# Ten operations for an inverse root, and other places for three writes and for four kinds of loads, in a fused S4 and gMLP kernel on one core

## The chip, the core and the metric

The kernel runs on one core of one Trainium2 chip. The core has a matrix engine (PE), a vector engine (DVE), an activation engine (ACT), a general engine (POOL) and a queue engine (SP). PE writes into eight accumulation banks (PSUM); DVE and ACT read the banks and work on the on-chip memory. Transfers to and from the chip's main memory are issued by SP, ACT or POOL and carried by 16 shared DMA engines. Every engine works through its own instructions in order and waits for the others by semaphores. The metric is the device time of one execution in microseconds.

## The reference, cut to what matters

```python
def _B_ref(x, w_in, w_sp, b_sp, w_out):
    z = _gelu(jnp.einsum("bsd,df->bsf", x, w_in))
    z1 = z[..., :Fh]
    z2 = _layernorm(z[..., Fh:], axis=-1)
    g = jnp.einsum("ts,bsf->btf", w_sp, z2) + b_sp[None, :, None]
    return jnp.einsum("bsf,fd->bsd", z1 * g, w_out)

mod = (_silu(c) @ w_mod).reshape(c.shape[0], 6, 1, -1)
sa, ca, ga, sb, cb, gb = (mod[:, 0], mod[:, 1], mod[:, 2], mod[:, 3], mod[:, 4], mod[:, 5])
h = _layernorm(x, axis=-1) * (1 + ca) + sa
x = x + ga * _A_ref(h, ...)          # S4: 576 channels, 128 poles each, a convolution over 2048 tokens
h = _layernorm(x, axis=-1) * (1 + cb) + sb
x = x + gb * _B_ref(h, ...)          # 2048 tokens, w_in 576 x 4608, w_sp 2048 x 2048, w_out 2304 x 576
```

Every layer norm is `(x - m) / sqrt(v + 1e-5)`: the inverse root is what `rsqrt` computes.

## The kernel before

**Stages.** The first stage (`ssm`) computes the S4 branch; its order is a list written out by hand (`ORDER`). It writes x1, the input of the second half, to main memory (`x1_d`, shown as `x_d`) by channel chunks; the last 64 channels of tokens block 4 to 15 also stay on chip in `x1l`. The **token stage** (`phase_a`) takes the 2048 tokens in 16 blocks of 128: layer norm, transpose, product with the z2 half of w_in (`z2_mm`, five parts per block), GELU, the mean and variance of z2 over all 2304 columns (`z2_stats`), its inverse root (`roots`), the normed z2 (`z2_norm`) and its store (`z2_store`, shown as `z_d<-z`). Beside these run pieces of work that the third stage needs (`side`): w_in's z1 half is scaled, split in two 16-bit parts and stored (`win_d`), w_sp and w_out are measured, and the first seven of the eight w_sp row blocks of token block 0 are split into a high and a low part (`wsp_hi` on ACT, `wsp_lo` on DVE). The **third stage** (`phase_b`) takes the output tokens in four blocks of 512. In each, z1 is computed, w_sp is multiplied with z2 (`g_products`: products of sums in the manner of Strassen, each operand split in two 16-bit parts, so that three products stand for one), the gate is formed, and w_out is applied (`out_block`).

**What sets the order.** In the token stage and the third stage DVE, ACT, PE and SP follow the order in which the Python code issues instructions; POOL is free. `tied` means just that. The token loop runs in a fixed pattern per block; `side(b, k, ...)` hangs a piece of work at place k of block b: LD at its start, V0 after the first statistics, A1 after the third product, V1 before the last statistics.

**The end of the token stage.** After block 15 come `z2_stats(15, 5)`, `roots(15)`, `z2_norm(15)` and `z2_store(15)`. Then the first block of the third stage starts: five units of z1 (`z1_unit`, 14 products each, with a tile `wf` that `z1_load` brings from `win_d`; four tiles stand ready, the fifth takes the place of the first when that has been used), then `g_products` with sets of z2 (`z2_load` into a buffer `raw`, `z2_sums` on DVE, `z2_hi` on ACT, `z2_lo` on DVE into `zset`). There are four buffers `raw` and three `zset`.

**The change to the second block.** `out_block` goes over eight halves n = 0..7 (two column halves of four token tiles). For each it takes the next section of the generator `next_steps`, issues 54 products of w_out into two banks, and has the result summed (`out_sum`: one ACT copy, then three DVE operations on `ot`, the last of which also reads the x1 tile `xo` or `gt`; after every second one ACT issues the store to `out`). The sums of halves 0 to 2 come together after half 2, and the halves 1 and 2 take no section: there are six calls, and six sections. The sections prepare the next block: sums of the w_sp row blocks 1 to 7 (`step_sums(n, ("b", i))`, on DVE, with the ACT split behind them), their low parts (`step_lo`), their loads (`block_read`), and, for the second block alone (n = 1), the first set of the z1 weights (`("w", 0)`: loaded by `item_load`, four transfers of 128 KB, into `raw`; split into `zset`), and loads of further sets (`item_load`, a call that does nothing for n = 2 and 3). A buffer goes to the request that follows the earliest release in program order.

**rsqrt.** It starts from an integer estimate and takes three Newton steps, each instruction waiting for the one before, on tiles of 1 to 4 columns. It is called four times in `ssm` (`ln_stats`), once for the first three token blocks (`ln2_three`), and 16 times by `roots`.

In the trace, `bsz` are the statistics of z2, `vh`, `rq` and `rx` the tiles of `rsqrt`, `xz` the w_sp row blocks of the token stage, `nt` the transposed normed tokens, `ps` and `pz` the banks. Since a helper records every instruction of DVE, ACT, PE and SP, all have line L224.

Of the kernel before, what the change touches and what calls it, by code (L numbers as in the profile page):

```python
# [14 lines left out]
ALU = mybir.AluOpType  # L15
# [3 lines left out]
D = 576  # L19
# [8 lines left out]
CHL = CHW[-1]  # L28
# [872 lines left out]
def rsqrt(V, pool, r, var, n):  # L901

    vh = pool.tile([128, n], F32, name="vh%d" % n)
    q = pool.tile([128, n], F32, name="rq%d" % n)
    V.tensor_scalar(vh, var, 1e-5, 0.5, op0=ALU.add, op1=ALU.mult)
    V.tensor_single_scalar(q.bitcast(I32), vh.bitcast(I32), 1, op=ALU.logical_shift_right)
    V.tensor_scalar(r.bitcast(I32), q.bitcast(I32), -1, 0x5F3759DF - 0x400000, op0=ALU.mult, op1=ALU.add)

    for i in range(3):
        V.tensor_tensor(q, r, r, op=ALU.mult)  # L910
        V.tensor_tensor(q, q, vh, op=ALU.mult)
        if i < 2:
            V.scalar_tensor_tensor(r, q, 1.5, r, op0=ALU.subtract, op1=ALU.mult)
    V.tensor_scalar(q, q, -1.0, 1.5, op0=ALU.mult, op1=ALU.add)
    V.tensor_tensor(r, r, q, op=ALU.mult)


class Mixed:
# [7 lines left out]
class Mlp:  # L926
# [376 lines left out]

    def x1_load(self, b):
        xt = self.xts[b] = self.ap.tile([128, D], F32, name="x1t")
        self.nc.sync.dma_start(xt[:, :D - CHL], self.x1_d[b, :, :D - CHL])

    def ln2_stats(self, b, mv=None):
        V, ap = self.nc.vector, self.ap
        if b < 4:  # L1310
            self.xts[b] = self.x1f[:, b]
        else:
            V.tensor_copy(self.xts[b][:, D - CHL:], self.x1l[:, b - 4])
        x = self.xts[b]
        bs = ap.tile([128, 2, 6], F32, name="bsx")
        mv = self.mvx[b] = ap.tile([128, 2, 2], F32, name="mvx") if mv is None else mv
        for h in range(2):
            V.bn_stats(bs[:, h], x[:, 288 * h:288 * h + 288])
        V.bn_aggr(mv[:, 0], bs)
# [102 lines left out]
    def phase_a(self):  # L1422
# [16 lines left out]
        LD, PE, A0, A1, V0, V1 = range(6)  # L1439
        sides = [[[] for _ in range(6)] for _ in range(17)]  # L1440

        def side(b, k, fn, *a):
            sides[b][k].append((fn, a))
# [31 lines left out]
        for i in range(7):  # L1475
            side(9 + i, V0, self.wsp_sums, i)
            side(9 + i, A1, self.wsp_hi, 0, i)
            side(9 + i, V1, self.wsp_lo, 0, i)
            side(8 + i, V1, self.block_load, 0, i)
        side(12, LD, self.z1_rows, 0)  # L1480
        side(14, LD, self.bias_load, 0)
        for f, b in ((0, 14), (9, 15), (1, 15), (10, 15)):
            side(b, LD, self.z1_load, 0, f)


# [71 lines left out]
        cpa.close()  # L1557
        self.z2_stats(15, 5)
        self.roots(15)
        self.z2_norm(15)  # L1560
        self.z2_store(15)
        self.nc = plain
# [319 lines left out]
    def out_block(self, q, steps):  # L1882


        nc = self.nc
        A, S = nc.scalar, nc.sync
        halves = [(tt, h) for tt in range(4) for h in range(2)]
        pms = {}
        for n, (tt, h) in enumerate(halves):
            if n not in (1, 2):  # L1890
                next(steps)
            pms[tt, h] = [self.bank()[:, :288] for _ in range(2)]
            self.out_products(pms[tt, h], q, tt, h, range(8) if n < 3 else range(9))
            for k in range(3) if n == 2 else () if n < 2 else (n,):
                tt, h = halves[k]
                if n == 2:
                    self.out_products(pms[tt, h], q, tt, h, (8,))
                xt = self.wss["x", tt]
                self.out_sum(pms[tt, h], xt, q, h)
                b, hs = 4 * q + tt, slice(288 * h, 288 * h + 288)  # L1900
                if h == 1:
                    A.dma_start(self.out[b], xt)

    def last_products(self, pm, k, s, fs):
        T = self.nc.tensor
        pa, pl = pm
        for f in fs:
            p, w = self.prods[3, f][k], self.wlast(k, f)
            c, st, sp = slice(128 * s, 128 * s + 128), f == 0, f == 8
            T.matmul(pl, p[:, 1, c], w[:, 0], start=st, stop=sp)  # L1910
            T.matmul(pa, p[:, 0, c], w[:, 0], start=st, stop=False)
            T.matmul(pa, p[:, 0, c], w[:, 1], start=False, stop=sp)
# [145 lines left out]
    def next_steps(self, q, pg):  # L2058

        n = q + 1  # L2060
        gate = self.g_unit(q, 8, pg, 2)
        gate[0]()
        self.scale_gate(q)
        gate[1]()
        gate[2]()
        if q < 3:
            self.n2_adds(1, self.wss["n2", 1])
            self.block_read(n, 3)
        gate[3]()
        gate[4]()  # L2070
        if q == 3:
            return
        self.bias_load(n)
        self.step_hi(n, 1)
        self.step_sums(n, ("b", 1))
        self.rows_load(q, 1)
        self.step_lo(n, ("n", 1))
        self.step_sums(n, ("b", 2))
        self.step_lo(n, ("b", 1))
        self.block_read(n, 4)  # L2080
        self.block_read(n, 5)
        self.wr_scale(0)
        if n > 1:
            self.feed(n, 0)
            self.feed(n, 1)
        yield
        self.step_sums(n, ("b", 3))
        self.step_lo(n, ("b", 2))
        self.block_read(n, 6)
        self.step_sums(n, ("b", 4))  # L2090
        self.step_lo(n, ("b", 3))
        self.block_read(n, 7)
        self.rows_load(q, 2)
        yield
        self.step_sums(n, ("b", 5))
        self.step_lo(n, ("b", 4))
        self.item_load(n)
        yield
        self.step_sums(n, ("w", 0) if n == 1 else ("b", 6))
        self.step_lo(n, ("b", 5))  # L2100
        self.item_load(n)
        self.rows_load(q, 3)
        yield
        if n == 1:
            self.step_sums(n, ("b", 6))
            self.step_lo(n, ("w", 0))
        self.step_sums(n, ("b", 7))
        self.step_lo(n, ("b", 6))
        if n == 1:
            self.item_load(n)  # L2110
            self.feed(n, 1)
        yield
        self.step_lo(n, ("b", 7))
        self.item_load(n)
        self.item_load(n)
        self.item_sums(n, 3)
        yield
# [344 lines left out]
```

## Time and profile before

| what | value |
|---|---|
| runs | 1701.16, 1702.41 and 1707.59 us, median 1702.41 us |
| the profiled execution | 1696.56 us, of which 1694.1 us are the span |
| PE busy | 1620.3 us of the span |
| DVE busy | 1308.0 us |
| ACT busy | 873.0 us |
| moved by DMA | 380.35 MB, 225 GB/s on average |
| granted PE clock, mean | 0.986 |

The stages, by the time from the span's start: the first stage to about 384 us, the token stage to about 613 us, the first block of the third stage to about 889 us, and three more blocks to the end. The profile's columns: the time at which an instruction (or a run of like ones) starts, its duration, the engine, the operation, the tile that is written and those that are read, the shape; in square brackets, how long the engine had been idle before and what ended the wait. PEld is PE's load of weights, SPq and ACTq are queue instructions.

### The profile page before, as it was taken

To read this page: it belongs to the slowest core of one execution; us is meant where nothing else is said; L and a number is where in the kernel's file an instruction comes from. 1 tells how busy PE (TensorE), PEld (TensorE's weight loads), DVE (VectorE), ACT (ScalarE), POOL (GpSimd) and SP (SyncE) were. 2 spreads that over 40 slices of the span, in tenths; PEclk is the share of its full clock that TensorE was granted. 3 is DMA by queue.
4 is the path that set the end of the run, shared out by engine and by line. 5 is a ranking of instruction groups with operands and counts; after the bars stand their busy time and mean duration, and the time that the engine had idled before them with its cause. 6 is when DMAs were issued, how large, how long until landed. Compare 5 with 4: busy or idle time off the path is not lost.

```text
span 1694.1 us, 39997 instructions
## 1 busy us (share of the span) xinstructions
PE 1620.3 (96%) x16868; PEld 1238.2 (73%) x16868; DVE 1308.0 (77%) x2312; ACT 873.0 (52%) x1307; POOL 210.1 (12%) x340
## 2 busy tenths in 40 slices
PE   3788999989999999999999999999999999999999
PEld 1345677755555557778878888888888888888887
DVE  7998999867999977988987777785443387787555
ACT  6989999665776664554443533332321133353221
POOL 3261111112222110000000000000111100111100
PEclk9878999999999999999999999999999999999999
DMA  9667645696988788676748877665667573777560
GB/s 242 178 214 224 198 143 179 174 308 196 281 278 251 237 260 300 242 274 227 248 126 281 292 275 258 221 208 189 224 213 242 190 227 121 270 283 253 191 237 29
DMA packets 186402, 380.35 MB, mean 225 GB/s; under 512 B 38464, under 2 KB 105792, under 8 KB 185456
## 3 DMA queue, kind: packets, MB, share of 16 engines
q1 hardware_dynamic: 145216, 181.84, 35.0%
q0 software_dynamic: 34528, 169.11, 29.7%
q10 hardware_dynamic: 6480, 26.86, 4.0%
q8 instruction: 132, 2.16, 0.5%
q14 instruction: 46, 0.38, 0.1%
HBM read 272.47 MB, written 105.29 MB: 223 GB/s over the span
## 4 chain that ended last, share of the span: by engine, by line
PE 37%; issue 31%; DVE 12%; ACT 4%; DMA 4%; POOL 3%; SPq 0%; ACTq 0%; POOLq 0%; DVEq 0%
PE ps L224 21%; PE pz L224 10%; POOL zset L2158 3%; DMA zset<-set_d 2%; PE pk_b L224 2%; DVE zset L224 2%; PE pk_a L224 2%; DVE raw L224 1%; PE pk_c L224 1%; DVE gt L224 1%; PE pk_d L224 1%; DVE wsp L224 1%; DVE bsz L224 1%; ACT wsp L224 1%; DVE ot L224 1%
## 5 line engine op out<-in xcount | busy, mean ns | idle before, releaser
L224 PEld LDWEIGHTS <-zset 128*128 128x128 f16 x7182 | 701.8, 98 | 91.7 <-DVE zset L224 4.6
L224 PE MATMUL ps<-wsp,zset 128*128 128x256 f16 x6048 | 667.7, 273 | 4.0 <-DVE ot L224 1.5
L224 PE MATMUL pz<-wz,nt 128*128 128x512 f16 (+1 forms) x1120 | 220.9, 358 | 2.1 <-DVE nt L224 0.9
L224 ACT ACTIVATE z<-gt 128x1024 f16<-128x1024 f32 x56 | 59.0, 1054 | 255.9 <-DVE gt L224 255.9
L224 PEld LDWEIGHTS <-nt 128*128 128x128 f16 x1120 | 109.3, 98 | 107.9 <-DVE nt L224 1.8
L2158 POOL DMA_DIRECT2D zset<-set_d x96 | 50.8, 529 | 865.0 <-PE ps L224 614.8
L224 DVE SCALAR_TENSOR_TENSOR gt<-ps,sc,bsp 128x512 f32<-128x512 f32 x36 | 27.0, 749 | 144.5 <-PE ps L224 142.8
L224 PE MATMUL ps<-wout,z 128*128 128x288 f16 x1092 | 138.4, 286 | 0.0
L224 PEld LDWEIGHTS <-z 128*128 128x128 f16 x1176 | 115.1, 98 | 28.9
L224 DVE TENSOR_TENSOR raw<-raw 128x256 f32<-128x256 f32 (+3 forms) x238 | 126.8, 539 | 11.0 <-DMA raw<-z_d 4.1
L224 PE MATMUL ps<-n2o,zset 128*128 128x256 f16 x1134 | 128.4, 273 | 1.8 <-DVE zset L224 1.8
L224 DVE SCALAR_TENSOR_TENSOR gt<-ps,sc,gt 128x512 f32<-128x512 f32 (+1 forms) x180 | 122.2, 696 | 7.9 <-DVE gt L224 0.5
L224 ACT ACTIVATE zset<-raw 128x1792 f16<-128x1792 f32 x48 | 81.0, 1690 | 55.9 <-PE ps L224 17.8
L224 DVE TENSOR_TENSOR zset<-raw,zset 128x1792 f16<-128x1792 f32 x48 | 96.9, 2019 | 16.1 <-ACT zset L224 16.1
L224 DVE TENSOR_TENSOR z<-ps,z 128x512 f32<-128x512 f32 (+1 forms) x126 | 71.9, 598 | 36.3 <-ACT z L224 24.2
L224 ACT ACTIVATE z<-pz,sc 128x512 f32<-128x512 f32 (+1 forms) x96 | 51.2, 574 | 33.9 <-PE pz L224 19.5
L224 ACT ACTIVATE wsp<-raw,sc 128x1792 f16<-128x1792 f32 x25 | 44.6, 1784 | 46.2 <-DVE raw L224 37.2
L224 ACT ACTIVATE z<-z,sc 128x1024 f32<-128x1024 f32 x21 | 24.1, 1149 | 76.0 <-DVE z L224 72.2
L224 ACT ACTIVATE z1b<-gt 128x512 f16<-128x512 f32 (+1 forms) x22 | 17.7, 821 | 85.3 <-DVE gt L224 85.3
L224 PE MATMUL ps<-n2q,wf 128*128 128x512 f16 x252 | 55.9, 379 | 1.2 <-DMA wf<-win_d 1.2
L224 DVE SCALAR_TENSOR_TENSOR wsp<-raw,sc,wsp 128x1792 f16<-128x1792 f32 x25 | 51.9, 2077 | 0.0
L224 POOL DMA_DIRECT2D z_d<-z x32 | 32.2, 1006 | 150.7 <-ACT z L224 149.7
(795 smaller groups left out, 2813.2 us busy)
## 6 DMA issues: line engine op xcount, KB each, us to landing
zset<-set_d POOLq DMA_DIRECT2D x96, 896.0 KB, 5.3
raw<-z_d SPq DMA_DIRECT2D x48, 512.0 KB, 5.6
set_d<-zset ACTq DMA_DIRECT2D x24, 896.0 KB, 6.4
z_d<-z POOLq DMA_DIRECT2D x32, 576.0 KB, 8.8
zset<-wa_d POOLq DMA_DIRECT2D x18, 896.0 KB, 4.8
raw<-in_w_spT SPq DMA_DIRECT2D x25, 512.0 KB, 4.3
set_d<-zset SPq DMA_DIRECT2D x12, 896.0 KB, 5.9
wst<-in_w_in SPq DMA_DIRECT2D x8, 1024.0 KB, 9.5
```

Source lines behind the costliest of these rows:

```text
L224: return self.tc.keep_in_program_order(f(*a, **k))
L2158: self.nc.gpsimd.dma_start(o, self.set_d[f, j - 1] if j else self.wa_d[f])
```

## The change

Five things change.

1. `rsqrt` makes its first two Newton steps in one of higher order and then one Newton step: ten operations instead of thirteen.
2. Token blocks 8 to 15 load all 576 columns of x1 from main memory; the copy of 64 columns from `x1l` on DVE remains for blocks 4 to 7 alone. Eight copies go.
3. The low part of w_sp row block 6, the last that the token stage splits (`wsp_lo(0, 6)`), moves from its place V1 in block 15 to behind `roots(15)`.
4. The first four `z1_load` are asked for at blocks 12, 13, 13 and 14 instead of 14, 15, 15 and 15.
5. `next_steps` gets a seventh section, which `out_block` takes after its last sum. Row block 7 is loaded one section later, and its low part and the sums of set 3 come in the seventh section. For the second block the first z1 weights are asked for earlier, and their low part is made right behind the low part of row block 5.

```diff
@@ -906,13 +906,13 @@
     V.tensor_single_scalar(q.bitcast(I32), vh.bitcast(I32), 1, op=ALU.logical_shift_right)
     V.tensor_scalar(r.bitcast(I32), q.bitcast(I32), -1, 0x5F3759DF - 0x400000, op0=ALU.mult, op1=ALU.add)
 
-    for i in range(3):
-        V.tensor_tensor(q, r, r, op=ALU.mult)
-        V.tensor_tensor(q, q, vh, op=ALU.mult)
-        if i < 2:
-            V.scalar_tensor_tensor(r, q, 1.5, r, op0=ALU.subtract, op1=ALU.mult)
-    V.tensor_scalar(q, q, -1.0, 1.5, op0=ALU.mult, op1=ALU.add)
-    V.tensor_tensor(r, r, q, op=ALU.mult)
+    V.tensor_tensor(q, r, r, op=ALU.mult)
+    V.scalar_tensor_tensor(q, q, math.sqrt(1.5), vh, op0=ALU.mult, op1=ALU.mult)
+    V.scalar_tensor_tensor(q, q, 2.5 / math.sqrt(1.5), q, op0=ALU.subtract, op1=ALU.mult)
+    V.scalar_tensor_tensor(r, q, 1.875, r, op0=ALU.add, op1=ALU.mult)
+    V.tensor_tensor(q, r, r, op=ALU.mult)
+    V.scalar_tensor_tensor(q, q, -1.0, vh, op0=ALU.mult, op1=ALU.mult)
+    V.scalar_tensor_tensor(r, q, 1.5, r, op0=ALU.add, op1=ALU.mult)
 
 
 class Mixed:
@@ -1303,13 +1303,14 @@
 
     def x1_load(self, b):
         xt = self.xts[b] = self.ap.tile([128, D], F32, name="x1t")
-        self.nc.sync.dma_start(xt[:, :D - CHL], self.x1_d[b, :, :D - CHL])
+        n = D if b >= 8 else D - CHL
+        self.nc.sync.dma_start(xt[:, :n], self.x1_d[b, :, :n])
 
     def ln2_stats(self, b, mv=None):
         V, ap = self.nc.vector, self.ap
         if b < 4:
             self.xts[b] = self.x1f[:, b]
-        else:
+        elif b < 8:
             V.tensor_copy(self.xts[b][:, D - CHL:], self.x1l[:, b - 4])
         x = self.xts[b]
         bs = ap.tile([128, 2, 6], F32, name="bsx")
@@ -1475,11 +1476,12 @@
         for i in range(7):
             side(9 + i, V0, self.wsp_sums, i)
             side(9 + i, A1, self.wsp_hi, 0, i)
-            side(9 + i, V1, self.wsp_lo, 0, i)
+            if i < 6:
+                side(9 + i, V1, self.wsp_lo, 0, i)
             side(8 + i, V1, self.block_load, 0, i)
         side(12, LD, self.z1_rows, 0)
         side(14, LD, self.bias_load, 0)
-        for f, b in ((0, 14), (9, 15), (1, 15), (10, 15)):
+        for f, b in ((0, 12), (9, 13), (1, 13), (10, 14)):
             side(b, LD, self.z1_load, 0, f)
 
 
@@ -1557,6 +1559,7 @@
         cpa.close()
         self.z2_stats(15, 5)
         self.roots(15)
+        self.wsp_lo(0, 6)
         self.z2_norm(15)
         self.z2_store(15)
         self.nc = plain
@@ -1900,6 +1903,7 @@
                 b, hs = 4 * q + tt, slice(288 * h, 288 * h + 288)
                 if h == 1:
                     A.dma_start(self.out[b], xt)
+        next(steps)
 
     def last_products(self, pm, k, s, fs):
         T = self.nc.tensor
@@ -2089,29 +2093,31 @@
         self.block_read(n, 6)
         self.step_sums(n, ("b", 4))
         self.step_lo(n, ("b", 3))
-        self.block_read(n, 7)
+        self.item_load(n)
         self.rows_load(q, 2)
         yield
         self.step_sums(n, ("b", 5))
         self.step_lo(n, ("b", 4))
-        self.item_load(n)
+        self.block_read(n, 7)
         yield
         self.step_sums(n, ("w", 0) if n == 1 else ("b", 6))
         self.step_lo(n, ("b", 5))
-        self.item_load(n)
+        if n == 1:
+            self.step_lo(n, ("w", 0))
+            self.item_load(n)
         self.rows_load(q, 3)
         yield
         if n == 1:
             self.step_sums(n, ("b", 6))
-            self.step_lo(n, ("w", 0))
         self.step_sums(n, ("b", 7))
         self.step_lo(n, ("b", 6))
         if n == 1:
             self.item_load(n)
+            self.item_load(n)
             self.feed(n, 1)
         yield
+        yield
         self.step_lo(n, ("b", 7))
-        self.item_load(n)
         self.item_load(n)
         self.item_sums(n, 3)
         yield
```

What stands in a row on the engines that the prediction speaks of, at three places:

DVE at the end of the token stage, before: the statistics of block 15 (`bsz`), the low part of the w_sp row block 6 (`wsp<-xz`), the last two statistics, and the start of the last `rsqrt`.

```order
L224 BN_STATS bsz<-z_7713 128x6
L224 BN_STATS bsz<-z_7714 128x6
L224 SCALAR_TENSOR_TENSOR wsp<-xz,sc,wsp 128x7x256
L224 BN_STATS bsz<-z_7714 128x6 x2
L224 BN_AGGR mvx<-bsz 128x2
L224 TENSOR_SCALAR vh_7826<-mvx 128x1
```

DVE at the same place now, from the middle of the last `rsqrt` on; `r` and `nm` are the scale and shift that `z2_norm(15)` reads, and `raw` the sums of the first set of z2.

```order
L224 TENSOR_TENSOR rq_7758<-rx 128x1
L224 SCALAR_TENSOR_TENSOR rq_7758<-rq_7758,vh_7757 128x1
L224 SCALAR_TENSOR_TENSOR rx<-rq_7758,rx 128x1
L224 TENSOR_SCALAR r_7769<-rx 128x1
L224 SCALAR_TENSOR_TENSOR nm_7770<-mvx,r_7769 128x1
L224 SCALAR_TENSOR_TENSOR wsp<-xz,sc,wsp 128x7x256
L224 TENSOR_TENSOR raw<-raw 128x256
L224 TENSOR_TENSOR raw<-raw 128x512
```

The low part has moved from ahead of the last statistics to between the last `rsqrt` and the first sums of z2.

DVE at the change to the second block, before: the low part of row block 6, the sum of half 6, the low part of row block 7, the sums of set 3 and the sum of half 7.

```order
L224 SCALAR_TENSOR_TENSOR wsp<-raw,sc,wsp 128x7x256
L224 TENSOR_TENSOR ot<-ot,ps 128x288
L224 TENSOR_TENSOR ot<-ot,gbs 128x288
L224 TENSOR_TENSOR gt<-ot,gt 128x288
L224 SCALAR_TENSOR_TENSOR wsp<-raw,sc,wsp 128x7x256
L224 TENSOR_TENSOR raw<-raw 128x256
L224 TENSOR_TENSOR raw<-raw 128x512
L224 TENSOR_TENSOR ot<-ot,ps 128x288
L224 TENSOR_TENSOR ot<-ot,gbs 128x288
L224 TENSOR_TENSOR gt<-ot,gt 128x288
```

The same place now.

```order
L224 SCALAR_TENSOR_TENSOR wsp<-raw,sc,wsp 128x7x256
L224 TENSOR_TENSOR ot<-ot,ps 128x288
L224 TENSOR_TENSOR ot<-ot,gbs 128x288
L224 TENSOR_TENSOR gt<-ot,gt 128x288
L224 TENSOR_TENSOR ot<-ot,ps 128x288
L224 TENSOR_TENSOR ot<-ot,gbs 128x288
L224 TENSOR_TENSOR gt<-ot,gt 128x288
L224 SCALAR_TENSOR_TENSOR wsp<-raw,sc,wsp 128x7x256
L224 TENSOR_TENSOR raw<-raw 128x256
L224 TENSOR_TENSOR raw<-raw 128x512
```

The two sums of halves 6 and 7 follow each other, and row block 7's low part and set 3's sums come behind them. Earlier on the same engine, the low part of the first z1 weights (`zset<-raw,sc,zset`) now stands right behind the low part of row block 5, ahead of the sum of half 5 and the sums of row block 6.

SP at the change to the second block, before (-) and now (+): `in_w_spT` are row blocks of w_sp, `in_w_in` the z1 weights, `x_d` the x1 tiles, `wa_d` the store of the split z1 weights, `z_d` a set of z2.

```order
-L224 DMA raw<-in_w_spT 128x2x512 x4
-L224 DMA xo<-x_d 128x576
-L224 DMA raw<-in_w_in 128x2x128 x4
-L224 DMA raw<-z_d 128x1024
-L224 DMA gt<-x_d 128x576
-L224 DMA wa_d<-zset 128x3584
+L224 DMA raw<-in_w_spT 128x2x512 x3
+L224 DMA raw<-in_w_in 128x2x128 x4
+L224 DMA xo<-x_d 128x576
+L224 DMA raw<-in_w_spT 128x2x512
+L224 DMA wa_d<-zset 128x3584
+L224 DMA raw<-z_d 128x1024
```

The z1 weights now come ahead of the x1 tile `xo` and of the last row block. PE, ACT and POOL execute what they executed, in the same order.

## The prediction

> **What bounds the kernel now.** I read the head of the page first, then the table of stretches (columns: stretch, its length, busy us and instructions of PE, PEld, DVE, ACT and POOL, granted clock, DMA share, GB/s), then the timeline at the stretches in which PE is not full.
>
> ```profile
> span 1694.1 us, 39997 instructions
> PE 1620.3 (96%) x16868; PEld 1238.2 (73%) x16868; DVE 1308.0 (77%) x2312; ACT 873.0 (52%) x1307; POOL 210.1 (12%) x340
> ...
> PEclk9878999999999999999999999999999999999999
> ```
>
> ```profile
> 42.00:384.00 342.00, 308.02 (x6301) 206.96 (x6299) 304.16 (x482) 297.31 (x534) 80.06 (x126) 0.93 0.68 202
> 384.00:556.00 172.00, 171.39 (x916) 90.26 (x917) 156.21 (x478) 118.68 (x192) 40.58 (x55) 1.00 0.80 250
> 556.00:645.00 89.00, 86.72 (x498) 48.32 (x497) 74.15 (x191) 55.09 (x73) 12.25 (x14) 1.00 0.85 261
> 645.00:836.00 191.00, 190.05 (x1565) 152.72 (x1564) 165.91 (x195) 92.12 (x83) 0.57 (x1) 1.00 0.74 256
> 836.00:900.00 64.00, 60.72 (x500) 48.68 (x499) 57.44 (x84) 24.94 (x25) 0.55 (x1) 1.00 0.51 164
> 900.00:1094.00 194.00, 192.84 (x1747) 170.40 (x1746) 142.96 (x189) 77.71 (x93) 11.63 (x22) 1.00 0.80 275
> 1094.00:1694.00 600.00, 595.84 (x5271) 515.32 (x5268) 376.02 (x606) 178.74 (x259) 47.58 (x90) 1.00 0.60 204
> ```
>
> PE bounds the kernel: it is idle for 1694.1 - 1620.3 = 73.8 us in all, and no PE instruction is added or removed. The most that the edits can bring is the idle time of PE where they work: 89.00 - 86.72 = 2.28 us at the end of the token stage (556 to 645) and 64.00 - 60.72 = 3.28 us at the change to the second block (836 to 900). Before 556 PE is full, so the roots and copies there are hidden. Only in the first stage is something else open: PE, DVE and ACT are all at 87 to 90% from 42 to 384.
>
> **Cost of one root.** The rows are one of the 16 calls of `roots` (its first operation, its last, and the one that follows) and the start of the last call.
>
> ```profile
> 565.04 0.17 DVE L224 TENSOR_SCALAR vh<-mvx 128x2 f32<-128x2 f32 x1
> ...
> 567.42 0.16 DVE L224 TENSOR_TENSOR rx<-rx,rq 128x2 f32<-128x2 f32 x1
> 567.61 0.15 DVE L224 TENSOR_SCALAR r<-rx 128x1 f32<-128x1 f32 x1
> ...
> 620.76 0.15 DVE L224 TENSOR_SCALAR vh<-mvx 128x1 f32<-128x1 f32 x1
> ```
>
> Thirteen operations take 567.61 - 565.04 = 2.57 us, 0.198 us each, chained. I price the new fused operations at the same pitch, since the fused ones in this run (`rx<-rq,rx`) keep it too. Three fewer give **0.59 us** a call. [...]
>
> **End of the token stage.**
>
> ```profile
> PE pz L224 <- DVE nt L224: 0.9, 2, 0.5
> ```
>
> ```profile
> 560.63 0.18 DVE L224 COPY x1t<-x1l 128x64 f32<-128x64 f32 x1
> 560.72 0.81 DVE L224 BATCH_NORM_STATS2 bsx<-x1t 128x6 f32<-128x288 f32 x2
> ...
> 607.35 1.41 SPq L224 DMA_DIRECT2D wf<-win_d  x3
> ...
> 616.43 0.32 SPq L224 DMA_DIRECT2D wf<-win_d  x1
> ...
> 617.36 2.08 DVE L224 SCALAR_TENSOR_TENSOR wsp<-xz,sc,wsp 128x1792 f16<-128x1792 f32 x1 [1.12 <-ACT wsp L224]
> ...
> 623.71 2.59 ACT L224 ACTIVATE z<-z,nm,r 128x1152 f32<-128x1152 f32 x2 [5.44 <-DVE nm L224]
> ...
> 626.71 3.20 PE L224 MATMUL ps<-n2q,wf 128*128 128x512 f16 x14 [1.25 <-DMA wf<-win_d]
> ...
> 627.91 2.03 DVE L224 TENSOR_TENSOR zset<-raw,zset 128x1792 f16<-128x1792 f32 x1 [3.24 <-ACT zset L224]
> ...
> 634.23 0.32 SPq L224 DMA_DIRECT2D raw<-z_d  x1
> ```
>
> From 556 on the chain of waits runs through DVE and ACT, not PE, so their savings add up there. Five calls of `roots` start from there on, one a token block, the first and the last those of 565.04 and 620.76: 5 x 0.59 = 2.95 us. Two of the eight copies lie here; the next instruction starts 0.09 us after one starts, so they bring 0.2 us. DVE then reaches `nt` over 0.6 us earlier at its two waits (0.6 us for the first: the roots of 565 and the copy of 561), and the **0.9 us** that PE waits for `nt` go. The fifth `wf` was issued at 616.43, when the first had been used, and landed at about 626.7, behind three others issued at 607.35 on the same queue. These three, 0.96 MB, leave that place; at the stretch's 261 GB/s they are 3.7 us of traffic, more than the **1.25 us** that PE waits. PE then starts the first z2 products some 2.2 us earlier, at 629.9 - 2.2 = 627.7.
>
> What would be late next is the first `zset`. Its sums stand behind the moved write as they did before, so that move is neutral for them, and they come 2.95 + 0.2 = 3.1 us earlier: the DVE write of 627.91 starts at 624.8 and ends at 626.8, 0.9 us ahead of PE. The norm of block 15 gains 2.08 us more, less what it then waits for its GELU (between 0 and 1.1 us), so the set load blocked until 634.23 by the store goes out some 4 us earlier. Without that cover each microsecond of a late set costs PE one. Term: **2.3 us**, the whole idle time; bounds 0.9 (only the `nt` waits go) and 2.3. The wider x1 loads are 8 x 32 KB more, below 1 us of DMA spread over eight blocks, on a core whose DMA share is 0.80: nothing.
>
> **Change to the second block.**
>
> ```profile
> 874.29 0.42 SPq L224 DMA_DIRECT2D xo<-x_d  x1
> ...
> 878.99 1.91 SPq L224 DMA_DIRECT2D raw<-in_w_in  x4
> ...
> 882.53 0.89 DVE L224 TENSOR_TENSOR raw<-raw 128x256 f32<-128x256 f32 x2 [2.02 <-DMA raw<-in_w_in]
> ...
> 889.24 2.08 DVE L224 SCALAR_TENSOR_TENSOR zset<-raw,sc,zset 128x1792 f16<-128x1792 f32 x1
> ...
> 891.37 4.54 PE L224 MATMUL ps<-n2o,zset 128*128 128x256 f16 x40 [1.80 <-DVE zset L224]
> ...
> 896.35 2.08 DVE L224 SCALAR_TENSOR_TENSOR wsp<-raw,sc,wsp 128x1792 f16<-128x1792 f32 x1
> ...
> 899.40 0.45 DVE L224 TENSOR_TENSOR ot<-ot,ps 128x288 f32<-128x288 f32 x1
> 899.90 5.29 PE L224 MATMUL ps<-wsp,zset 128*128 128x256 f16 x47 [1.48 <-DVE ot L224]
> 900.37 0.46 DVE L224 TENSOR_TENSOR gt<-ot,gt 128x288 f32<-128x288 f32 x1
> ...
> 901.38 1.70 ACT L224 ACTIVATE zset<-raw 128x1792 f16<-128x1792 f32 x1 [6.13 <-DMA raw<-in_w_in]
> ...
> xo<-x_d SPq DMA_DIRECT2D x1, 288.0 KB, 4.3
> ```
>
> Here DVE is the late one: it waits 2.02 us for the z1 weights, and PE waits 1.80 us for their low part and 1.48 us for a bank that the sum of half 7 holds. The weights are now asked for after row block 3's low part instead of row block 4's, 5 us earlier (at about 874 by the `xo` row, which followed at the same release), so the 2.02 us go. Their low part also passes the sum of half 5 (1.4 us) and row block 6's sums (1.5 us): 889.24 - 2.02 - 2.9 = 884.3, done at 886.4, 3 us before PE asks at 889.6. The 1.80 us go. The sum of half 7 passes row block 7's low part and set 3's sums (899.40 - 896.35 = 3.05 us): 899.40 - 2.02 - 3.05 = 894.3, its bank free at 894.8. PE, 1.80 us earlier, wants it at 896.6: the 1.48 us go too. Queued behind: `xo` is issued 1.9 us later, behind the four (1.91 us of issue), and lands 4.3 us after that, at 874.3 + 1.9 + 4.3 = 880.5, about when DVE reads it; a stall there of up to 0.5 us lies inside these margins. Late next is set 3: its ACT part stood at 901.38, behind the store of half 7; now its sums end at about 899 and its low part at 902.9 (1.70 and 2.02 us), while PE wants it about 84 products after 894.8, at some 904: a margin of 1 us. Term: **3.3 us**, bounds 2.0 (only DVE's wait is won) and 3.3.
>
> At the other two changes the moved write costs nothing, because DVE waits there:
>
> ```profile
> 1162.26 0.45 DVE L224 TENSOR_TENSOR ot<-ot,ps 128x288 f32<-128x288 f32 x1 [1.51 <-ACT ot L224]
> ```
>
> **First stage.**
>
> ```profile
> L224 DVE TENSOR_TENSOR rq<-rq,vh x15: 161/161/164, 26.8 to 376.4; 128x4 f32<-128x4 f32 x12, 128x3 f32<-128x3 f32 x3
> ...
> 384.25 1.02 DVE L224 TENSOR_TENSOR nt<-pt,nt 128x512 f16<-128x512 f32 x2 [5.14 <-ACT nt L224]
> ...
> 140.00:160.00 20.00, 18.07 (x529) 11.25 (x528) 14.22 (x18) 19.22 (x39) 2.81 (x4) 0.88 0.67 214
> ```
>
> The product with `vh` comes three times a call: four calls on 4 columns, 4 x 0.59 = 2.4 us of DVE. The call on 3 columns ends ahead of DVE's pause of 5.14 us and brings nothing. From 140 to 160 ACT is the full engine and DVE waits, so part is lost; bounds 0 and 2.4, and I take **1.0**.
>
> **Sum.** 2.3 + 3.3 + 1.0 = 6.6 us. The profiled execution took 1696.56 us (span plus 2.5), so its like would take 1690.0. The runs shown lie higher, at a median of 1702.41; the forecast is 1702.4 - 6.6 = **1695.8 us**, 0.39% less. A measurement tells about 0.5%, or 8.5 us, from no change. Bounds of the terms: 0.9 + 2.0 + 0 = 2.9 to 2.3 + 3.3 + 2.4 = 8.0 us.
>
> **Rivals.** (a) *Everything comes through*: the first stage gives its 2.4 us, and of the 1.16 us of PE's idle time from 900 to 1094 (waits for sets) some goes too: 8.0 to 9.2 us, about 1694 us. For it: DVE is above 90% busy in most of the first stage. Against: ACT and PE are too. Chance 0.17. (b) *Traffic, not order, is late*: the fifth `wf` and the sets wait for bytes, and moving three loads changes nothing.
>
> ```profile
> 612.00:620.00 8.00, 8.00 (x45) 4.21 (x44) 6.38 (x11) 5.83 (x7) 2.00 (x2) 1.00 1.06 329
> ```
>
> The DMA engines are full there. Then 1.25 us stay, and set 3's margin breaks as well: 0.9 + 2.0 = 2.9 to 4 us, about 1699. Against: the three loads leave this stretch for one where the share is lower. [...] Chance 0.15. (c) *The clock takes it back*: the granted clock was 0.93 from 42 to 384 and 1.00 after; were the fuller PE throttled by 1% over the 1049 us from 645 on, it would lose 10.5 us, and the time would be 1706, slower. It decides from 0.6%. Against: PE is full from 645 to 836 at 1.00. Chance 0.05. (d) *The edits don't reach PE*: DVE is held by ACT at both places, and nothing beyond 1 us is won, 1701.5. Chance 0.06. The forecast, 4 to 8 us, has 0.57.
>
> The range takes in (a), (b) and most of (d), and the runs' spread: 1689 to 1702. Faster by over 0.5%: (a) and a little of the forecast, 0.20. Slower: 0.04. Within: 0.76.
>
> **What would show it.** Right: no PE wait for `nt` or `wf` between 550 and 640, none for `zset` or `ot` around 890, no DVE wait for `in_w_in`, ten operations at 0.198 us. Wrong: a PE wait for `zset` in the first products of either block, DVE waiting for `xo` at half 4, a clock below 1.00 after 340, or a first stage that ends later than 384.

## The result, and the profile after

| | runs | median | lowest to highest |
|---|---|---|---|
| before | 6 | 1703.03 us | 1701.16 to 1707.59 us |
| changed | 6 | 1693.95 us | 1691.0 to 1697.43 us |

The ratio is 0.995 (95% interval 0.9932 to 0.9968), so 9.1 us less, or 5.4 to 11.6 us by the interval. The forecast was 1695.8 us, 6.6 us less. A second set of runs of the same kernel gave 1694.37 us beside 1704.19 us, a ratio of 0.9951 (0.9935 to 0.9967).

The profiled execution took 1691.0 us. The head of its page, and then its table of the same stretches as before (length, busy us and instructions of PE, PEld, DVE, ACT and POOL, granted clock, DMA share, GB/s):

```profile
span 1688.9 us, 39922 instructions
...
PE 1615.6 (96%) x16868; PEld 1235.7 (73%) x16868; DVE 1298.4 (77%) x2241; ACT 873.8 (52%) x1307; POOL 209.7 (12%) x340
```

```profile
42.00:384.00 342.00, 304.30 (x6308) 203.66 (x6306) 302.54 (x470) 296.54 (x532) 78.26 (x124) 0.95 0.68 202
384.00:556.00 172.00, 170.48 (x906) 89.40 (x907) 151.69 (x440) 118.33 (x191) 40.18 (x55) 1.00 0.82 255
556.00:645.00 89.00, 88.70 (x518) 50.56 (x517) 72.80 (x173) 57.92 (x77) 14.26 (x16) 1.00 0.91 268
645.00:836.00 191.00, 190.03 (x1569) 153.07 (x1568) 165.39 (x196) 91.32 (x83) 0.60 (x2) 1.00 0.73 253
836.00:900.00 64.00, 64.00 (x535) 52.08 (x533) 57.34 (x84) 26.79 (x28) 1.04 (x2) 1.00 0.54 170
900.00:1094.00 194.00, 192.81 (x1749) 170.58 (x1748) 146.15 (x194) 78.68 (x94) 11.10 (x21) 1.00 0.79 272
1094.00:1689.00 595.00, 590.86 (x5227) 511.08 (x5224) 371.74 (x600) 175.95 (x256) 47.58 (x90) 1.00 0.60 205
```

PE's idle time has gone from 2.28 us to 89.00 - 88.70 = 0.30 us at the end of the token stage and from 3.28 us to nothing at the change to the second block. From 645 to 836 and behind 900 it is as before. Ahead of 556 it is longer (37.70 us for 33.98 from 42 to 384, and 1.52 for 0.61 from 384 to 556): the first stage lies otherwise in this execution, as shown below. DVE has 71 instructions fewer: 63 of the 21 roots and eight copies.

The spans alone differ by 5.2 us, the medians by 9.1 us. To see why, I cut each trace at three points of PE: the first z2 product (the end of the first stage), and the first w_out product of the first and of the second block. The rows of the timeline (start, duration, engine, operation, tiles, shape, count) are, of before and then of the changed kernel:

```profile
384.10 2.76 PE L224 MATMUL pz<-wz,nt 128*128 128x512 f16 x12 [0.69 <-ACT nt L224]
...
836.27 0.90 PE L224 MATMUL ps<-wout,z 128*128 128x288 f16 x6
...
1108.94 2.25 PE L224 MATMUL ps<-wout,z 128*128 128x288 f16 x17
```

```profile
385.78 1.04 PE L224 MATMUL pz<-wz,nt 128*128 128x512 f16 x4 [0.69 <-ACT nt L224]
...
835.23 2.00 PE L224 MATMUL ps<-wout,z 128*128 128x288 f16 x15
...
1104.13 1.14 PE L224 MATMUL ps<-wout,z 128*128 128x288 f16 x8
```

All kernels of this study, cut in the same way, in us (the last column is the sum of the three stretches behind the first stage):

| kernel | first stage ends | token stage and first block | change to the second block | rest | behind the first stage |
|---|---|---|---|---|---|
| before | 384.10 | 452.17 | 272.67 | 585.17 | 1310.0 |
| changed | 385.78 | 449.45 | 268.90 | 584.78 | 1303.1 |
| changed, again (e5) | 388.87 | 449.00 | 268.59 | 584.98 | 1302.6 |
| e1, roots alone | 386.26 | 448.97 | 272.70 | 585.05 | 1306.7 |
| e2, second block alone | 388.74 | 452.25 | 268.77 | 585.11 | 1306.1 |
| e3, loads alone | 396.26 | 452.24 | 272.03 | 584.88 | 1309.2 |
| e4, roots and loads | 389.67 | 449.01 | 271.42 | 584.90 | 1305.3 |
| e6, without copies and moved write | 389.77 | 449.40 | 268.84 | 584.96 | 1303.2 |
| e7, old roots in first stage | 390.40 | 450.87 | 270.31 | 584.77 | 1306.0 |
| e8, long roots in first stage | 397.05 | 448.99 | 268.23 | 584.88 | 1302.1 |
| e9, early load alone | 394.25 | 452.45 | 269.32 | 584.91 | 1306.7 |
| e10, order without it | 389.55 | 453.37 | 270.37 | 584.78 | 1308.5 |
| e11, roots and second block | 387.83 | 448.99 | 268.74 | 584.77 | 1302.5 |
| e12, loads behind | 389.42 | 448.98 | 269.97 | 585.47 | 1304.4 |

Behind the first stage the change brings 1310.0 - 1303.1 = 6.9 us: 2.7 in the first block, 3.8 at the second, 0.4 in the rest. The first stage itself ended 1.7 us later in the changed kernel's trace. It is the stage that differs most from execution to execution: the profiled execution of before, at 384.1, has the shortest first stage of all 14 traces, and its 1696.56 us lie below all six timed runs. So the spans show less than the medians.

What the root, the first sets and the second block look like now, in rows of the timeline of the changed kernel (the start and the end of one root, PE's five z1 units and the first z2 sets, then the second block):

```profile
578.91 0.17 DVE L224 TENSOR_SCALAR vh<-mvx 128x2 f32<-128x2 f32 x1
...
580.89 0.15 DVE L224 TENSOR_SCALAR r<-rx 128x1 f32<-128x1 f32 x1
...
614.15 15.27 PE L224 MATMUL ps<-n2q,wf 128*128 128x512 f16 x70
...
626.20 2.02 DVE L224 TENSOR_TENSOR zset<-raw,zset 128x1792 f16<-128x1792 f32 x1 [1.81 <-ACT zset L224]
...
629.26 3.00 PE L224 MATMUL ps<-wsp,zset 128*128 128x256 f16 x26
```

```profile
872.81 1.90 SPq L224 DMA_DIRECT2D raw<-in_w_in  x4
...
879.03 0.46 DVE L224 TENSOR_TENSOR xo<-ot,xo 128x288 f32<-128x288 f32 x1
...
882.99 2.08 DVE L224 SCALAR_TENSOR_TENSOR zset<-raw,sc,zset 128x1792 f16<-128x1792 f32 x1
...
888.15 4.75 PE L224 MATMUL ps<-n2o,zset 128*128 128x256 f16 x42
...
892.73 1.03 PE L224 MATMUL ps<-n2r,wr 128*128 128x256 f16 x6
893.02 0.46 DVE L224 TENSOR_TENSOR gt<-ot,gt 128x288 f32<-128x288 f32 x1 [0.28 <-DMA raw<-in_w_in]
893.40 0.45 DVE L224 TENSOR_TENSOR ot<-ot,ps 128x288 f32<-128x288 f32 x1
...
899.77 2.02 DVE L224 TENSOR_TENSOR zset<-raw,zset 128x1792 f16<-128x1792 f32 x1 [1.89 <-ACT zset L224]
```

The five units run without a gap, the first set is done at 626.20 + 2.02 = 628.22, 1.0 us before PE takes it, and the first products of the second block follow each other without a wait. The 0.28 us that DVE waits at 893.02 stand ahead of an operation that reads `gt` and not the z1 weights: `gt` was asked for at 886.0 and took 6.9 us to land, so it is the likely cause, though the profile names `in_w_in`.

### The profile page after: what moved, and what is told of

It is laid out like the page before. It is cut to its first block, busy times and chain, and to the rows that moved or that the text cites. A ratio compares the mean times of both kernels' runs of the same rounds, so it can differ in the third digit from the quotient of the medians.

```text
span 1688.9 us, 39922 instructions
## 1 busy us (share of the span) xinstructions
PE 1615.6 (96%) x16868; PEld 1235.7 (73%) x16868; DVE 1298.4 (77%) x2241; ACT 873.8 (52%) x1307; POOL 209.7 (12%) x340
## 4 chain that ended last, share of the span: by engine, by line
PE 77%; DVE 7%; DMA 3%; issue 2%; ACT 2%; SPq 0%; POOL 0%; ACTq 0%; DVEq 0%; POOLq 0%
PE ps L224 58%; PE pz L224 10%; PE pk_b L224 2%; PE pk_a L224 2%; DMA zset<-set_d 2%; PE pk_c L224 2%; PE pk_d L224 1%; DVE zset L224 1%; DVE gt L224 1%; DVE bsz L224 1%; PE ps_a L224 0%; PE ps_b L224 0%; DMA v_d<-v_a 0%; PE pt L224 0%; DMA uu_a<-in_x 0%
## 5 line engine op out<-in xcount | busy, mean ns | idle before, releaser
L224 DVE BATCH_NORM_STATS2 bsz<-z 128x6 f32<-128x384 f32 x96 | 48.4, 548 | 5.0 <-ACT z L224 4.4
```

What stands on the lines that cost most here:

```text
L224: return self.tc.keep_in_program_order(f(*a, **k))
```

## Experiments

### The end of the token stage: which part brings it (e1, e3, e4)

e1 has the ten-operation root alone, e3 the earlier loads alone, e4 both:

```diff
-        for f, b in ((0, 14), (9, 15), (1, 15), (10, 15)):
+        for f, b in ((0, 12), (9, 13), (1, 13), (10, 14)):
             side(b, LD, self.z1_load, 0, f)
```

> The kernel before with the ten-operation root alone. Measured from the token stage's first z2 product to the end of the span (before 1694.1 - 384.1 = 1310.0 us, after 1688.9 - 385.8 = 1303.1 us), where the clock was 1.00. Theory (the edits gain only as far as the next wait lets them): the two waits of PE for nt (0.9 us) go, the wait for the fifth wf (1.25 us) stays, since its place behind three loads on the queue is as before; it may even grow by what PE arrives earlier. So 1309.1 to 1310.0 us, and the second block's waits of 1.80 and 1.48 us stay. Rival (every operation saved from 556 on reaches PE): five calls of 0.59 us, 1307.0 us. For the whole time: a gain of 0 to 0.9 us there and of 0 to 2.4 us in the first stage, with 1.0 us as the value taken; 0.999 of before, not told apart from no change.

> The kernel before with the first four z1_load asked for at blocks 12, 13, 13, 14 alone. Theory (the next thing late is the first zset): the wait of 1.25 us for the fifth wf goes, PE reaches the first products of the sets 1.25 us earlier, at 628.7, and waits there for zset, whose write ends at 629.9 as before: nothing gained, 1310.0 us from the first z2 product to the end, with a PE wait for zset of 1.2 us. Rival (the order of the loads alone was late): 1308.7 us and no wait for zset. Rival (traffic, not order): the wf wait stays at 1.25 us, 1310.0 us without a wait for zset.

> The kernel before with the ten-operation root and the earlier z1_load together. Theory (each needs the other): the waits for nt (0.9 us) and for the fifth wf (1.25 us) go, and the first zset, five calls of 0.59 us earlier, is there in time: 2.15 us, 1307.8 us from the first z2 product to the end, without a PE wait for zset. Sum of the two alone by the theory: 0.9 us at most, so 1.25 us come only from both. Rival (traffic): 1309.1 us, the wf wait stays.

Measured: e1 1306.7 us behind the first stage, a gain of 3.3 us and nearer to the rival's 1307.0 than to the theory's 1309.1; e3 1309.2; e4 1305.3 for the 1307.8 expected. So the theories of e1 and e4 are out: the wait for `wf` did not stay in e1, and e4 does not need both parts. In whole time e1 is 1698.13 us, 0.9972 of before (0.9956 to 0.9989); e3 and e4 were executed once each. In the token stage and the first block, where this gain arrives, the table has 3.2 us for e1, nothing (-0.1 us) for e3 and 3.2 us for both together. The stretch from 556 to 645 of e1, and then e1's rows behind the token stage (PE and DVE):

```profile
556.00:645.00 89.00, 89.00 (x520) 50.92 (x519) 74.75 (x178) 57.01 (x74) 12.25 (x14) 1.00 0.89 276
```

```profile
614.16 15.27 PE L224 MATMUL ps<-n2q,wf 128*128 128x512 f16 x70
...
624.88 2.02 DVE L224 TENSOR_TENSOR zset<-raw,zset 128x1792 f16<-128x1792 f32 x1 [3.24 <-ACT zset L224]
...
629.27 3.00 PE L224 MATMUL ps<-wsp,zset 128*128 128x256 f16 x26
```

In this stretch PE is never idle, although the fifth `wf` still stood behind three others. The roots moved these as well. The rows are DVE's write that frees the buffer of the next `xz` load, and what SP then issues, of before (its three `wf` loads follow at 607.35) and of e1; SP's own waits name this write in both:

```profile
604.82 2.08 DVE L224 SCALAR_TENSOR_TENSOR wsp<-xz,sc,wsp 128x1792 f16<-128x1792 f32 x1 [0.93 <-ACT wsp L224]
...
606.93 0.37 SPq L224 DMA_DIRECT2D xz<-in_w_spT  x1
```

```profile
602.93 2.08 DVE L224 SCALAR_TENSOR_TENSOR wsp<-xz,sc,wsp 128x1792 f16<-128x1792 f32 x1 [0.93 <-ACT wsp L224]
...
605.46 1.42 SPq L224 DMA_DIRECT2D wf<-win_d  x3
```

Counted from the first z2 product, the three loads come 607.35 - 384.10 - (605.46 - 386.26) = 4.05 us earlier in e1, because DVE's write does, and PE's first unit only 1.2 us earlier. The fifth `wf` then landed 6.3 us after its issue, for 10.2 us in before. In e3 the five units run without a gap too, but the time is not won:

```profile
642.21 3.01 PE L224 MATMUL ps<-wsp,zset 128*128 128x256 f16 x26 [1.30 <-DVE zset L224]
```

PE waits 1.30 us for the first `zset` instead of 1.25 us for `wf`, as the theory of e3 had it. In before the fifth unit ends at 626.71 + 3.20 = 629.91 and the write of the first `zset` at 627.91 + 2.03 = 629.94, so the two were late by the same amount and the profile named only one of them. The other kernels with the old root in the token stage divide the wait between the two (`wf` and `zset` 0.24 and 0.89 us in e2, 0.39 and 0.75 in e9, 1.11 and 0 in e10), and the sum stays at 1.1 to 1.3 us. What was late was DVE; the roots alone bring the whole gain, and the moved loads bring none that shows.

### The change to the second block (e2, e9, e10)

e2 has the whole new order (part 5) in the kernel before. e9 has only the earlier load, e10 all but the earlier load:

```diff
         self.step_lo(n, ("b", 3))
-        self.block_read(n, 7)
+        self.item_load(n)
...
         self.step_lo(n, ("b", 4))
-        self.item_load(n)
+        self.block_read(n, 7)
```

> The kernel before with the new order at the change to the second block alone (seven sections, the earlier load of the first z1 weights, their low part behind row block 5's). Theory: PE's waits of 1.80 us (zset) and 1.48 us (ot) and DVE's 2.02 us for in_w_in go, 3.3 us, all of it kept to the end: from the first z2 product to the end 1306.7 us for 1310.0. The end of the token stage is as before (waits for nt 0.9 us, wf 1.25 us). Rival (the edits need each other: without the earlier token stage the loads of the third stage stand otherwise, and one of the waits comes back): 1308.2 us or more.

> The kernel before with one step of the second block's order alone: the first z1 weights are asked for one section earlier and row block 7 one later; six sections, the low part in its old place. Theory (the lower bound of the prediction's term, only DVE's wait is won): DVE's 2.02 us for in_w_in go, the low part is done when PE asks, so the wait of 1.80 us for zset goes; the sum of half 7 still stands behind row block 7's low part and the sums of set 3, so the wait for ot stays at about 1.4 us. From the first out product of the first block to that of the second block (before 724.84 - 452.17 = 272.7 us, after 718.33 - 449.43 = 268.9 us) 270.7 us. Rival (the order of the writes is what counts): 272.7 us, both waits stay.

> The counterpart: the kernel before with the seven sections and the new order of the writes, but the first z1 weights asked for in their old section. Theory (the order of the writes is what counts): DVE still waits about 2 us or more for in_w_in, but their low part no longer stands behind row block 6's sums and half 5's sum, so it is done at about the time PE asks, and the sum of half 7 comes some 3 us earlier; PE waits 0.5 us at most, and the same stretch takes 269.0 to 269.5 us. Rival (the load is what counts): a wait for zset of 1 us or more stays, 270.5 us or more.

Measured: e2 gains 3.9 us in this stretch (268.77 for 272.67) and 3.9 us behind the first stage, and keeps the waits of the token stage's end, about as long in sum. In time it is 1698.06 us, 0.9985 of before (0.9965 to 1.0005), which alone can't be told from no change. e9 takes 269.32 us, e10 270.37 us, each in one execution. PE's waits in this stretch (what is waited for, us in total, times, longest), of e9 and then of e10:

```profile
PE ps L224 <- DVE ot L224: 1.4, 1, 1.4
PE ps L224 <- DMA zset<-set_d: 0.4, 1, 0.4
```

```profile
PE ps L224 <- DMA zset<-set_d: 1.2, 2, 0.9
PE ps L224 <- ACT ot L224: 0.5, 1, 0.5
PE ps L224 <- DVE ot L224: 0.3, 1, 0.3
```

Of e9 the theory holds by its waits: the one for `zset` is gone, the one for `ot` stays at 1.4 us. The time is 1.4 us below the expected 270.7; 0.6 us of it are waits of PE for later z2 sets (`set_d`, 1.0 us in before, 0.4 here; called set waits below), and 0.7 us is PE's busy time (269.32 - 1.4 - 0.4 = 267.5 us for 268.2), which was shorter with fewer waits here too, as told in the last section. Of e10 it holds in part: DVE waits 2.27 us for the weights, and yet PE has no wait for `zset`:

```profile
889.54 0.89 DVE L224 TENSOR_TENSOR raw<-raw 128x256 f32<-128x256 f32 x2 [2.27 <-DMA raw<-in_w_in]
...
893.13 2.08 DVE L224 SCALAR_TENSOR_TENSOR zset<-raw,sc,zset 128x1792 f16<-128x1792 f32 x1
```

The low part ends at 895.2, and PE asks at 895.8. But 0.8 us of waits for `ot` are left where 0.5 us at most was expected, and with 1.2 us of set waits the time lies above the expected 269.0 to 269.5.

Either step alone takes the first wait away; only the order, not the load, shortens the second. By these traces both are needed for the full 3.8 us, and their single gains (3.4 and 2.3 us) do not add; with the set waits taken out of every trace they are 2.8 and 2.5 us, of 3.9.

### The first stage (e5, e7, e8)

e7 is the changed kernel with the old root at the four calls of `ssm`, e8 the changed kernel with this behind the new one there:

```diff
+    for i in range(20):
+        V.tensor_tensor(q, r, r, op=ALU.mult)
```

> The changed kernel once more, to see what of its trace comes again. From the token stage's first z2 product to the end the first trace has 1303.1 us, with a wait of PE for nt (ACT) of 0.3 us in token block 14, behind a wait of 5.9 us of ACT for a w_sp load (wsst) that two wf loads were issued ahead of. Theory (the earlier wf loads stand in front of that load in every run): the wait comes again, 1303.1 us. Rival (a delay of that one run): no such wait, 1302.6 us. The first stage ended at 385.8 us; it waits there for the loads of w_mod and on the clock, and may lie some us either way.

> The changed kernel with the thirteen-operation root at the four calls of the first stage alone. What comes behind the first stage is the changed kernel's, 1303.1 us. Theory of the prediction: the whole time is 1.0 us longer than the changed kernel's (bounds 0 and 2.4). Rival (the first stage's length is set by the loads of w_mod, by ACT and by the clock, and the roots there are hidden): no difference that can be told, 0.

> The changed kernel with twenty more operations behind the root (they write a tile that is not read) at the four calls of the first stage alone: 4 x 20 x 0.198 = 15.8 us more of DVE there. If an operation there costs 1.0/2.4 of its time, as the prediction took, the whole time is 6.6 us longer than the changed kernel's. Rival (DVE bounds the first stage): 15.8 us longer. Second rival (the roots there are hidden): 0 to 2 us longer.

| | median | ratio to before (95% interval) |
|---|---|---|
| e5 | 1694.37 us | 0.9951 (0.9935 to 0.9967) |
| e7 | 1696.08 us | 0.9954 (0.9938 to 0.9969) |
| e8 | 1704.21 us | 1.0007 (0.9993 to 1.0022) |

e8 is 9.8 us longer than e5 for 4 x 3.90 = 15.6 us more of DVE (each twenty take 3.90 us in its trace): 0.63 us for each. That is between the prediction's 0.42 and the rival's 1, but with some 2.6 us to either side of each median the share may lie anywhere between about 0.4 and 0.8, so 0.42 is not excluded. By this share the 2.4 us that the roots save there are worth 1.5 us, an estimate from e8; it supposes that operations taken out bring as much as operations put in cost, which no run shows. e7's difference, 1.7 us, agrees, but its two intervals overlap almost whole; taken alone it shows nothing. Nor need it come from the first stage: in e7's trace the part behind it takes 1306.0 us, 2.9 us more than in the changed kernel's.

e5's rival held: the wait for `nt` did not come again, and the trace has 1302.6 us. It came again in e7, as below.

### The earlier loads, the copies and the moved write (e6, e11, e12)

e6 is the changed kernel without parts 2 and 3, e11 the kernel before with parts 1 and 5 alone, e12 the changed kernel with the loads behind the w_sp loads of their block:

```diff
-            side(b, LD, self.z1_load, 0, f)
+            side(b, A1, self.z1_load, 0, f)
```

> The changed kernel with two of its five parts undone: the 64 columns are copied again for all of blocks 4 to 15 (and the x1 loads are as narrow as before), and the low part of row block 6 is made at its old place in block 15. Theory (these two parts bring nothing, and the wider loads add to the traffic ahead of the w_sp load): no wait of PE for nt in block 14, and from the first z2 product to the end the sum of what roots with loads and the second block brought alone, 4.7 + 3.8 = 8.5 us, 1301.5 us. Rival (the two parts are worth what the prediction's small terms say, a fifth of a us for the copies): 1303.3 us. Second rival (the wait in block 14 comes from the wf loads alone): it is here too, 1302.0 us or more.

> The kernel before with the ten-operation root and the second block's order, without the earlier wf loads, the wider x1 loads and the moved write. Theory (the two effects seen alone add up, 3.3 + 3.8 us, and the other three parts bring nothing): from the first z2 product to the end 1302.9 us, no wait for wf, and no ACT wait for the w_sp load (wsst) in block 14 above 1.5 us; the whole time that of the changed kernel. Rival (the earlier loads are needed now and then): a PE wait for the fifth wf of up to 1.25 us comes back, 1304.1 us.

> The changed kernel with its four earlier wf loads at place A1 of blocks 12 to 14 for LD, so that on SP each stands behind the two w_sp loads (wsst) of its block and no longer ahead of them. Theory (the wf loads ahead of wsst are what ACT, and now and then PE, waits for in block 14): ACT's wait for wsst there is 1.5 us at most, as without the earlier loads, PE has no wait for nt or wf, and from the first z2 product to the end it is 1302.5 us or less. Rival (traffic of any place delays wsst): an ACT wait of over 2 us for wsst stays in block 14 or 15.

The only PE wait that the token stage's end kept, in the changed kernel's trace, seems to come from the loads. Its timeline ahead of block 14:

```profile
578.10 0.88 SPq L224 DMA_DIRECT2D wf<-win_d  x2
...
579.07 5.87 SPq L224 DMA_DIRECT2D wsst<-in_w_spT  x2
...
583.38 1.06 ACT L224 ACTIVATE wsst<-wsst 128x1024 f32<-128x1024 f32 x1 [5.92 <-DMA wsst<-in_w_spT]
...
586.23 1.04 PE L224 MATMUL pz<-wz,nt 128*128 128x512 f16 x4 [0.30 <-ACT nt L224]
```

Two `wf` loads (0.64 MB) stand ahead of the w_sp loads on SP's queue, ACT waits 5.92 us for these, and its half of `nt` is late. With the loads behind them (e12):

```profile
581.28 1.06 ACT L224 ACTIVATE wsst<-wsst 128x1024 f32<-128x1024 f32 x1 [0.17 <-DMA wsst<-in_w_spT]
...
581.74 1.08 SPq L224 DMA_DIRECT2D wsst<-in_w_spT  x2
...
582.91 2.80 SPq L224 DMA_DIRECT2D wf<-win_d  x2
```

At this place ACT waits 0.2 us for `wsst` in e12, 1.3 us in e1 and not at all in e11, which both load late. In the kernels with the new root and the loads ahead it waited 5.9 us (changed), 2.7 (e5), 5.3 (e4), 2.3 (e6), 5.1 (e7) and 0 (e8); e3, with the old root and the loads ahead, has no such wait. PE felt it twice: 0.3 us, and 1.7 us in e7. The loads were moved, and the wait went; since e8 and e3 have none either, one trace of e12 makes this likely and does not settle it.

In time none of this shows. e6: 1303.2 us behind the first stage for the 1301.5 expected, which had added up two traces, one of them (e4) with few set waits; it lies at its first rival's 1303.3, but 0.5 us of it is a wait for a later `zset` and 0.5 us set waits, so a price for the copies can't be read from it; 1696.37 us, 0.995 (0.9935 to 0.9965). e11: 1302.5 us for 1302.9, no wait for `wf`; 1696.97 us, 0.9962 (0.995 to 0.9974). e12: 1304.4 us, not the 1302.5 expected, because 2.3 us of set waits fell into this execution, 1.2 us more than into the changed kernel's first; 1696.08 us, 0.9947 (0.9935 to 0.996). Parts 2, 3 and 4 bring nothing that can be measured, and no version is told apart from the changed kernel; with the runs of one kernel 5.1 us (e12) to 16.2 us (e2) apart, a difference of a microsecond or two would not show.

## Why the prediction was right, and where not

- **What bounds the kernel**: right. PE's idle time at the two places was what could be won there, and the granted clock stayed at 1.00 after 340 in the trace of the changed kernel (in e5's it was 0.95 from 350 to 384 and 1.00 from there).
- **Cost of one root**: right. From `vh` to the operation behind it 580.89 - 578.91 = 1.98 us for 2.57, 0.59 us. That is 0.198 us for each of the ten, the pitch at which the prediction priced them; the duration of the fused ones is 0.16 us, as that of the old ones was.
- **End of the token stage**, 2.3 us: measured 2.7 and 3.2 us (the changed kernel's two traces), 3.2 us in e1 and e4. The place of the first set came out: 626.20 is 240.42 us behind the first z2 product, for 240.7 predicted, and 1.0 us ahead of PE. The step that failed is the one that gave the 1.25 us of `wf` to the three moved loads ("These three, 0.96 MB, leave that place"). They did free that place: in e3 the wait for `wf` is gone. But e3 shows them to be worth nothing without the roots, e4 nothing beside them, and e1 that the roots alone end the wait, since they also bring the three loads 4 us forward. The prediction had the reason at hand: it named the first set as the next thing late, and in before it was as late as `wf`.
- **Earlier loads at no cost**: not quite. What was counted was the place that they leave; that they come to stand ahead of `wsst` was not. The sign "no PE wait for `nt`" was missed by the 0.3 us above, and by 1.7 us in e7.
- **Change to the second block**, 3.3 us: measured 3.8 and 4.1 us (two traces), 3.9 us alone (e2). Both waits and DVE's 2.02 us went. Measured from the first w_out product of the first block, the low part was done 0.3 us earlier than predicted, the sum of half 7 within 0.2 us, and the low part of set 3 at 902.8 for 902.9 in before's time. `xo` did not stall.
- **Both terms were 0.4 to 0.9 us too small**, for the larger part because idle time was counted at its face value. By the cuts of the table PE's busy time, which holds none of the idle time, fell as well, for the same products: by 0.8 and 0.9 us in the first stretch (448.43 us to 447.67 and 447.51, the changed kernel's two traces) and by 0.5 and 0.3 us in the second (268.22 to 267.71 and 267.95). In e5's second stretch the larger rest, 0.5 us, is shorter set waits. Behind the `zset` wait of 1.80 us the way from the first product of set 2 to the next group took 895.75 - 889.19 = 6.56 us in before and 892.73 - 888.15 = 4.58 us now, 1.98 us less.

```profile
889.19 0.38 PE L224 MATMUL ps<-n2o,zset 128*128 128x256 f16 x2
891.37 4.54 PE L224 MATMUL ps<-n2o,zset 128*128 128x256 f16 x40 [1.80 <-DVE zset L224]
895.75 0.60 PE L224 MATMUL ps<-n2r,wr 128*128 128x256 f16 x3
```

- **First stage**, 1.0 us: by e8 1.5 us, inside its bounds, and an estimate. The row from 140 to 160, from which the prediction took that part is lost, lies behind all four calls: they start at 25.91, 71.85, 101.56 and 127.42 us. From 60 to 140 of before DVE is busy for 76.29 us, 95%, and is the fullest engine (ACT 72.25, PE 63.41). The sign "a first stage that ends later than 384" came true (385.78 and 388.87 us) without the prediction being wrong; it was taken from the shortest first stage of all traces.
- **Sum**, 6.6 us: 2.7 + 3.8 + 0.4 + 1.5 = 8.4 us by the runs, beside 9.1 us of the medians and inside their interval, which also holds the forecast's 6.6; the medians alone could not tell these sums apart. The range of 1689 to 1702 us would have held any gain from 0.4 to 13.4 us, so that the time fell into it says little of the mechanism; the traces say more. Standing on the median and not on the profiled execution was right, since that had an unusually short first stage.
- **Rivals.** *Everything comes through* gave about 1694 us, and that is where the time fell, but not for its reasons: the first stage gave 1.5 and not 2.4 us, and the waits for sets after 900 stayed (1.2 and 1.1 us; 0.3 to 2.3 us over all traces, with no order in them). *Traffic, not order* is out, since the wait for `wf` went in e3, where the three loads alone were moved, and set 3 was in time. *The clock* and *the edits don't reach PE* are out.

## What to carry to other kernels

Where two things are late at the same moment, the profile may name one alone, as here (629.91 and 629.94 us); price the removal of a wait by the time at which the other would be ready, and look which part moves that. The earlier loads seem to have made late what they came to stand ahead of in their queue (ACT waited 5.92 us for `wsst` in the changed kernel's trace and 0.17 us in e12's, but not at all in e8's), so look there as well as at the place that a moved load leaves. Where one stage varies from run to run, cut the traces at fixed points and compare the stages behind it; they showed here what 0.2% of the time are made of, which the time alone did not.

## What was not expected of the hardware

Two waits of PE cost more than the idle time shown in front of them. The first cost 1.98 us for 1.80, by the rows above. The five z1 units of before took 629.75 - 613.22 = 16.53 us with the wait of 1.25 us, and 629.27 - 614.16 = 15.11 us in e1 without it, 1.42 us less. So each of these two waits cost about 0.2 us on top. The cause was not tested and stays open.

```profile
613.22 12.25 PE L224 MATMUL ps<-n2q,wf 128*128 128x512 f16 x56
...
629.75 10.45 PE L224 MATMUL ps<-wsp,zset 128*128 128x256 f16 x89
```

The first stage ended between 384.1 and 396.3 us in the traces without the extra operations of e8, far more than the edits explain. In the pair of before and changed, most of the difference arises between 37 and 48 us (the changed kernel is 1.2 us late before that), where PE works off the same groups of products at another pace; the rows are of before and then of the changed kernel:

```profile
41.03 1.16 PE L224 MATMUL pk_d<-k_a,ec 96*32 96x288 f32 x12 [1.06 <-DMA k_a<-in_w_mod]
...
43.10 0.75 PE L224 MATMUL pk_c<-mpart,small 128*128 128x288 f32 x2
```

```profile
43.61 2.13 PE L224 MATMUL pk_d<-k_a,ec 96*32 96x288 f32 x12 [1.39 <-DMA k_a<-in_w_mod]
...
47.50 1.33 PE L224 MATMUL pk_c<-mpart,small 128*128 128x288 f32 x2
```

Twelve products take 2.13 us for 1.16, two take 1.33 for 0.75. Both traces begin at the slow pace (two products `pk_b<-mpart,small` take 1.17 us at 37.58 in before and at 38.79 in the changed kernel's); it ends at about 39 us in before and at about 50 us in the changed kernel's, an estimate from such rows. The changed kernel is 4.4 us late at the last of these rows. More than half of that is won back by 384, with a granted clock of 0.95 for 0.93 from 42 to 384. The granted clock of the profile is 1.00 in both before 60 us and doesn't show this pace. What causes it is not shown, and what the phase does to the rest of the first stage stays open.
